# Fills on GpSimd, the bound of v from TensorE, one bank for the column products of w_in, and a written-out order made anew

## The chip, the core and the metric

The kernel runs on one core of a Trainium2 chip. The metric is the device time of one execution in microseconds (us), the median of three runs. The profile is of one further execution of the same program.

The engines are TensorE (PE in the profile; PEld its weight loads), VectorE (DVE), ScalarE (ACT), GpSimd (POOL) and SyncE (SP), which issues most DMAs. Each runs its own list of instructions strictly in order and waits for others by semaphores.

## The reference, cut to what matters

```
# q, k, v: 4 x 8 heads x 576 x 64
out_d  = softmax(q_d @ k_d.T / 8) @ v_d     # q_d, k_d, v_d: means over groups of 4 positions
local  = softmax(q @ k.T / 8, |i - j| < 4) @ v
x      = repeat(out_d, 4) + local           # 2304 tokens x 512
g      = relu(x @ w_in) ** 2                # w_in 512 x 2048
y      = g @ w_out                          # w_out 2048 x 512
logits = y @ w_gate + log1p(exp(y @ w_noise)) * noise
out    = sum over the two best of 8 experts e of weight * relu(y @ w1[e]) @ w2[e]
```

`w_in` and `w_out` come as 8-byte floats and are turned into 4-byte ones on the chip. Every product is made of 2-byte halves: each operand is scaled by a power of two and split into a high and a low fp16 part, and three products (high-high, high-low, low-high) are added. The scale needs a bound of the operand's size, so that nothing overflows: for x a bound from v (a mean of rows of v can't be larger than v), for w_in a bound of its columns, for w_out one of its norm.

## The kernel before, in words

A table `ORDER` of some 1100 short names sets the program: each name is a step with its number, `start` says which function it calls, and the steps are issued in the table's order. So each engine's list is the table's order, cut down to what each step puts on that engine.

The part of the program ahead of the first product of x with w_in is called **the start** here. It holds

- `constants()`: masks, identity matrices (`idf`, `idb`) and zero fills (`pms`, `pTs`, `vws`; VectorE, lines 159 to 162);
- units of attention, 8 for each of the 4 sequences. A unit loads `qkT` (step `qk`), sums groups of four (`G`, VectorE, L268), makes scores (`S` and `D`, TensorE, L295 and L310), takes maxima (`ml`, `md`, VectorE), exponentials (`el`, `ed`, ScalarE), sums and divisions (`nl`, `nd`; for the first sequence the multiplications of `nd` are GpSimd's), transposes (`PT`, TensorE and ScalarE), multiplies by v (`PW`, tile `px`, TensorE, then VectorE `xt` L448), and splits x (`xb`, tile `xall`);
- v's groups (`vg` loads, `vm` bounds, `vs` sums). `vm` for all sequences is two squares with a running sum on ScalarE (L215), 0.63 us each; `Xa`, `Xm`, `Xb` make the scale of x from it;
- the eight pieces of w_in: load (`il`), ScalarE (`ia`, L530), VectorE (`ib`, L538), ScalarE (`ic`, L542), VectorE (`ij`, L547), then the products of column blocks with themselves on TensorE (`in`, L1065) into four PSUM banks, `pn` twice and `pm` twice; four reductions on VectorE (`is`, L1071) and one over their results (`wS`, L1075) give the bound, `wT` and `wU` the scale `s_in`;
- the split of w_in into `wih` (`wh`, ScalarE, L1088) and `wil` (`wl`, VectorE, L1095), eight column blocks of each;
- the eight pieces of w_out in the same way; their norm is read by `os`: eight products of column blocks with themselves (L1120) and a multiplication by the identity with a sum (VectorE, L1121), then `of` (tile `pfr`).

Then come 72 steps `M` (x times w_in, tile `ph`, 24 matmuls each, L617), of which eight belong to one chunk of 256 tokens, and `Y` (g times w_out, tile `y`); the first chunk's are in quarters, `yh` and `yl`. Attention units 4 and later of the table, the gate of each of 18 tiles of 128 tokens (`ga` to `gg`) and the scatter of its rows lie between them. A gate is `ga`, `gb` (row of y), `gc` (its transpose), `gd` (logits, tile `pl`, TensorE), `gf` (some twenty small VectorE instructions: `gate_d2`, `gate_d3`, `gate_d4`), `ge` (ranks, tile `pr`, TensorE, which needs `ohs`, a late result of `gf`) and `gg`. The steps `cm` (tile `phc`, L932) and `cw` (`po`, L948) are the first expert's products, `pe` the preparation of the experts' weights; the loop over the experts 1 to 7 follows.

Of the kernel before, what the change touches and what calls it, by code (L numbers as in the profile page):

```python
# [26 lines left out]
P = 128  # L27
# [25 lines left out]
vg0 vg3 ob0 qk0 vg2 S0 vg1 vm0 qk1 qk2 vm1 vm2 G0 S1 ml0 G1 D0 md0 ml1 el0 vg4 ed0 S2 vm3 G2 vm4 el1 D1 il0 Xa0  # L53
md1 Xm0 nl0 nd0 D2 vw0 vs4 ed1 ia0 md2 PT0 nl1 ed2 nd1 ib0 Xb0 ml2 qk3 ic0 el2 G3 S4 vs0 il1 nl2 ia1 il2 ij0 PT1
nd2 ib1 PW0 il3 ic1 D4 S3 ia2 md4 ml3 il4 vw1 vs1 ed4 D3 el3 md3 ia3 il5 PT2 il6 ml4 S5 el4 ib2 ij1 ib3 D5 nl3
md5 vw2 nl4 in0 nd4 ed3 S6 xb0 in1 ia4 nd3 ic3 il7 ib4 PW1 ij3 ol2 D6 ic2 ij2 md6 in2 ic4 xb1 ia5 ij4 vs2 PT3
ib5 ia6 ic5 ib6 vs3 ml5 vw3 PW2 ol3 in3 ij5 ic6 ol0 xb2 vg5 ia7 ij6 vw4 in4 ib7 PT4 ic7 in5 oa2 is3 ij7 in6 ed5
oB2 PW3 in7 oa3 is7 el5 oc2 wS0 ml6 wT0 ol1 oj2 wU0 xb3 oa0 wh1 oB0 oB3 vw5 nl5 wh5 wl1 oc0 oj0 wh0 wl0 os0 wh3
oc3 oj3 oa1 qk4 oB1 os2 wl5 wh2 wl3 wh6 wh7 os3 el6 M5 oc1 oj1 qk5 wl7 ed6 of3 ra5 os1 wh4 nl6 M0 wl6 wl4 vm5
wl2 S7 r0 of1 PW4 nd5 oh2 oo2 ol5 oh3 oh0 vs5 oo3 M1 ra1 ol6 oh1 oo0 G4 D7 M4 ol7 PT5 xb4 nd6 yh0 yl9 M3 r4 md7  # L60
ra3 PW5 yl1 yl0 yh9 oa5 M6 oa6 oo1 yl13 oB5 ml7 ol4 xb5 r6 yl8 yl11 yl3 oa7 S8 yl12 PT6 yl4 ed7 el7 oB6 vg6 M2
oB7 yh6 yh8 ml8 oc5 nl7 yh4 M7 oj5 yh13 oc6 D8 oc7 oj6 yh11 oj7 yh3 oa4 vm6 yh1 oB4 os7 os5 yh14 vw6 md8 yl14
# [37 lines left out]
def moe_kernel(ctx, tc, qk_in, vwin, vgrp, w_in, w_out, w_gate, w_noise, noise, w1, w2, out):  # L100
# [940 lines left out]
    def win_pieces():  # L1041
# [343 lines left out]
```

## Time and profile before

| | |
|---|---|
| three runs | 974.52, 974.89, 978.32 us, median 974.89 |
| the profiled execution | 974.24 us, its span 972.5 us |
| TensorE busy | 916.3 us, 94% of the span |
| VectorE busy | 580.7 us, 60% |
| ScalarE busy | 498.9 us, 51% |
| GpSimd busy | 132.4 us, 14% |
[...]

The span runs from the first instruction to the last one in the trace; the execution's own time is 1.7 us longer. Busy shares are means over stages with different limits.

### The profile page before, as it was taken

Reading aid. Unit: us, or ns where it says so; the run is one execution under the profiler, and the core shown is the slowest. Engines: PE = TensorE matmul, PEld = TensorE weight load, DVE = VectorE, ACT = ScalarE, POOL = GpSimd, SP = SyncE. Lnnn points to the kernel's source line nnn. Section 1 sums busy time; section 2 is a strip of 40 time slices with the busy share of each in tenths; the row PEclk is TensorE's granted clock in tenths of the full one; section 3 lists DMA queues with packets and bytes.
Section 4 is the critical chain, followed back from the end, with each engine's and each line's share of the span. In section 5 each row is a group of like instructions: output and inputs, shape, how many; then the busy total and the mean of one; then the engine's idle time right before and its main releaser. Section 6 shows DMA issues by size and latency. Waiting matters only on the chain.

```text
span 972.5 us, 20336 instructions
## 1 busy us (share of the span) xinstructions
PE 916.3 (94%) x8278; PEld 619.0 (64%) x8278; DVE 580.7 (60%) x1812; ACT 498.9 (51%) x1076; POOL 132.4 (14%) x151
## 2 busy tenths in 40 slices
PE   4549999999999899999999979999999999999997
PEld 2437988675766567676757546746565565656574
DVE  7989887488678666566477765543435262626221
ACT  5688767455466455455744472753626263624010
POOL 2501100011102010010111121020111111110203
PEclk9768999999999999999999999999999999999999
DMA  9942587923241502013411748771847667590304
GB/s 290 337 147 97 169 262 287 240 90 86 88 101 58 86 30 49 21 61 96 161 56 36 226 122 222 122 206 20 221 56 204 73 187 90 158 119 10 43 1 55
DMA packets 103143, 121.17 MB, mean 125 GB/s; under 512 B 68256, under 2 KB 68448, under 8 KB 100992
## 3 DMA queue, kind: packets, MB, share of 16 engines
q1 hardware_dynamic: 94544, 100.30, 38.0%
q0 software_dynamic: 8496, 19.48, 10.0%
q8 instruction: 67, 1.10, 0.5%
q14 instruction: 36, 0.29, 0.1%
HBM read 70.33 MB, written 35.02 MB: 108 GB/s over the span
## 4 chain that ended last, share of the span: by engine, by line
PE 65%; DVE 4%; ACT 2%; DMA 1%; issue 0%; POOL 0%; POOLq 0%; ACTq 0%; DVEq 0%
PE po L948 20%; PE phc L932 19%; PE y L663 11%; PE ph L617 11%; DMA xs<-row,si 1%; ACT xall L861 1%; PE px L429 1%; PE px L421 1%; PE pol L975 1%; PE S L310 0%; PE S L295 0%; PE pfr L479 0%; PE ptp L375 0%; PE pl L740 0%; ACT r L636 0%
## 5 line engine op out<-in xcount | busy, mean ns | idle before, releaser
L617 PE MATMUL ph<-xall,wih 128*128 128x256 f16 x1152 | 196.1, 276 | 0.6 <-ACT r L636 0.4
L932 PEld LDWEIGHTS <-we 128*128 128x128 f16 x1536 | 148.5, 98 | 50.7
L948 PE MATMUL po<-we,h 128*128 128x512 f16 (+1 forms) x816 | 177.3, 379 | 0.0
L617 PE MATMUL ph<-xall,wil 128*128 128x256 f16 x576 | 158.6, 275 | 2.0 <-DVE wil L1095 2.0
L932 PE MATMUL phc<-xT,we 128*128 128x384 f16 (+1 forms) x1152 | 150.6, 293 | 0.0
L948 PEld LDWEIGHTS <-h 128*128 128x128 f16 (+1 forms) x816 | 83.4, 102 | 91.2
L663 PE MATMUL y<-wo,gh 128*128 128x512 f16 x448 | 133.3, 379 | 0.0
L617 PEld LDWEIGHTS <-wih 128*128 128x128 f16 x1152 | 111.1, 99 | 18.4 <-issue 1.9
L934 ACT ACTIVATE h<-phc 128x384 f16<-128x384 f32 (+1 forms) x112 | 47.3, 423 | 135.3 <-PE phc L932 135.3
L950 DVE TENSOR_SCALAR ob<-po,om 128x512 f32<-128x512 f32 (+1 forms) x34 | 25.5, 749 | 122.8 <-PE po L948 122.8
L832 POOL DMA_INDIRECT xs<-row,si x36 | 38.6, 1072 | 403.1 <-issue 110.3
L951 POOL DMA_INDIRECT out_dram<-ob,tk x34 | 52.3, 1538 | 298.6 <-DVE ob L950 284.2
L935 DVE SCALAR_TENSOR_TENSOR h<-phc,h 128x384 f16<-128x384 f32 (+1 forms) x112 | 52.2, 470 | 64.9 <-ACT h L934 64.9
L663 PE MATMUL y<-wo,gl 128*128 128x512 f16 x224 | 84.9, 379 | 0.3 <-DVE gl L646 0.3
L663 PEld LDWEIGHTS <-gh 128*128 128x128 f16 x448 | 42.1, 98 | 44.6 <-issue 1.0
L646 DVE TENSOR_TENSOR gl<-g,gh 128x512 f16<-128x512 f32 x64 | 44.3, 693 | 39.7 <-ACT gh L645 39.3
L617 PEld LDWEIGHTS <-wil 128*128 128x128 f16 x576 | 56.9, 99 | 9.8 <-DVE wil L1095 2.5
L636 ACT ACTIVATE r<-ph 128x512 f32<-128x512 f32 x72 | 42.2, 586 | 13.2 <-PE ph L617 13.0
L640 ACT ACTIVATE g<-r 128x512 f32<-128x512 f32 x72 | 45.4, 630 | 2.3
L861 ACT ACTIVATE junk<-w1raw 128x1024 bf16<-128x1024 f32 x24 | 25.4, 1056 | 36.4 <-DMA w1raw<-in_moe_w_dram 25.8
L878 DVE SCALAR_TENSOR_TENSOR we<-w1raw,sce,we 128x1024 f16<-128x1024 f32 x32 | 40.6, 1278 | 2.7 <-ACT we L877 2.7
L878 DVE SCALAR_TENSOR_TENSOR we<-w2raw,sce,we 128x1024 f16<-128x1024 f32 x32 | 40.6, 1275 | 0.9 <-ACT we L877 0.9
(354 smaller groups left out, 1382.3 us busy)
## 6 DMA issues: line engine op xcount, KB each, us to landing
w1raw<-in_moe_w_dram SPq DMA_DIRECT2D x8, 2048.0 KB
w2raw<-in_moe_w_dram SPq DMA_DIRECT2D x8, 2048.0 KB
xs<-zrow SPq DMA_DIRECT2D x8, 1290.0 KB
qkT<-in_qk_dram SPq DMA_DIRECT2D x16, 579.0 KB
raw<-in_moe_w_out_dram SPq DMA_DIRECT2D x8, 1024.0 KB
out_dram<-zrow SPq DMA_DIRECT2D x1, 4864.0 KB
raw<-in_moe_w_in_dram SPq DMA_DIRECT2D x4, 1024.0 KB
vw<-in_vwin_dram SPq DMA_DIRECT2D x48, 76.0 KB
```

The lines of the kernel that those rows point to most:

```text
L617: nc.tensor.matmul(ph[:, f], a[:, kk, fo], bb[:, kk], start=(n == 0), stop=(n == 11))
L636: nc.scalar.activation(r, ph, AF.Relu, scale=KAPPA)
L640: nc.scalar.activation(g, r, AF.Square)
L646: nc.vector.tensor_tensor(gl, g, gh, op=OP.subtract)
L663: nc.tensor.matmul(py[c, tt], a[:, o], bb[:, ft], start=(ft == 0 and n == 0), stop=(ft == 15 and n == 2))
L832: st = nc.gpsimd.indirect_dma_start(out=xs, out_offset=bass.IndirectOffsetOnAxis(ap=si[:, kk:kk + 1], axis=0), in_=roww, in_offset=None)
L878: nc.vector.scalar_tensor_tensor(wl[:, o], raws[i][:, o], ss[i], wh[:, o], op0=OP.mult, op1=OP.subtract)
L932: nc.tensor.matmul(ph[:, :n], a[:, fo], xT[:, bb], start=(i == 0), stop=(i == 11))
L934: nc.scalar.activation(hh[:, f], ph[:, :n], AF.Relu)
L935: nc.vector.scalar_tensor_tensor(hl[:, f], ph[:, :n], 0.0, hh[:, f], op0=OP.max, op1=OP.subtract)
L948: nc.tensor.matmul(po, a[:, f, jo], bb[:, do], start=(i == 0), stop=(i == 23))
L951: st = nc.gpsimd.indirect_dma_start(out=out, out_offset=bass.IndirectOffsetOnAxis(ap=tk[:m], axis=0), in_=ob[:m], in_offset=None, compute_ ...
```

## The change

Six things change.

1. The zero fills of `pms[1]`, `pTs` and `vws` are GpSimd's.
2. For the first sequence, `vm` is eight matmuls on TensorE: the upper halves of v's 4-byte words, read as 2-byte floats, in blocks of 128 columns times themselves, added up in one bank `pv0`, 32 matmuls in all. The largest element bounds v. The other sequences keep ScalarE's squares. `x_scale(0)` reduces `pv0` instead of `vmx`.
3. w_in's 64 products of column blocks go into one bank `pn`, on top of each other, and one reduction reads it (`is7`; the other `is` do nothing). `wS` has no reduction left.
4. w_out's norm per piece is the largest element of the products (one reduction) in place of the sum of the diagonal.
5. `gf` of the tiles 0 to 15 is three steps, `gx`, `gy`, `gz`, so that other steps can stand between.
6. `ORDER` is new from the first name to the last.

```diff
-vg0 vg3 ob0 qk0 vg2 S0 vg1 vm0 qk1 qk2 vm1 vm2 G0 S1 ml0 G1 D0 md0 ml1 el0 vg4 ed0 S2 vm3 G2 vm4 el1 D1 il0 Xa0
+qk0 vg0 G0 qk1 S0 S1 ml0 D0 G1 il0 el0 nl0 vg2 qk2 D1 ml1 md0 ed0 vm0 nd0 vg4 md1 ia0 vg1 el1 S2 ed1 ib0 S4 G2
...
         nc.gpsimd.memset(pms[0], 0.0)
+        for i in range(2):
+            nc.gpsimd.memset(pTs[i][0], 0.0)
+            nc.gpsimd.memset(vws[i][32:64], 0.0)
...
-        nc.vector.memset(pms[1], 0.0)
-        for i in range(2):
-            nc.vector.memset(pTs[i][0], 0.0)
-            nc.vector.memset(vws[i][32:64], 0.0)
+        nc.gpsimd.memset(pms[1], 0.0)
...
+    pv0 = ps1.tile([P, 512], F32, tag="m1", name="pv0")
+    seen_v = [0]
+
     def vg_max(b, hp):
+
         vg = vgs[b, hp]
-        for i in range(2):
...
+        if b:
+            for i in range(2):
...
+            return
+        v = vg.rearrange("g a b -> g (a b)").bitcast(BF16).rearrange("g (f n w) -> g f n w", n=P, w=2)[:, :, :, 1]
+        for f in range(8):
+            nc.tensor.matmul(pv0[:, :P], v[:, f], v[:, f], start=(seen_v[0] == 0), stop=(seen_v[0] == 31))
+            seen_v[0] += 1
...
-        nc.vector.tensor_reduce(m1, vmx[b], AX.X, OP.max)
+        nc.vector.tensor_reduce(m1, vmx[b] if b else pv0[:, :P], AX.X, OP.max)
...
-                nc.tensor.matmul(pn[i][:, P * (f % 4):P * (f % 4) + P], v[:, f], v[:, f], start=i in fresh,
-                                 stop=done_[i] == 16)
-                fresh.discard(i)
+                done_[0] += 1
+                nc.tensor.matmul(pn[:, P * (f % 4):P * (f % 4) + P], v[:, f], v[:, f], start=done_[0] == 1,
+                                 stop=done_[0] == 64)
 
         def peak(c):
-            for i in (2 * c, 2 * c + 1):
-                nc.vector.tensor_reduce(top[:, i:i + 1], pn[i], AX.X, OP.max)
+            if c:
+                nc.vector.tensor_reduce(top, pn, AX.X, OP.max)
...
-                nc.vector.scalar_tensor_tensor(pq[:, P:2 * P], pq[:, :P], 1.0, idf, op0=OP.mult, op1=OP.mult,
-                                               accum_out=acc[q_][:, c:c + 1])
+                nc.vector.tensor_reduce(acc[q_][:, c:c + 1], pq[:, :P], AX.X, OP.max)
```

Three places of the new order. First SyncE's list, the program's first loads (`wih` here is v's groups of the first sequence, four loads; `raw` a piece of w_in; `vw` v for the windows). Before:

```order
L206 DMA wih_168<-in_vgrp_dram 72x1024 x2
L251 DMA qkT0_0_186<-in_qk_dram 128x1158
L206 DMA wih_168<-in_vgrp_dram 72x1024 x2
L251 DMA qkT0_1_213<-in_qk_dram 128x1158
L251 DMA qkT0_2_215<-in_qk_dram 128x1158
L206 DMA vg1_0_262<-in_vgrp_dram 72x1024
L526 DMA raw_296<-in_moe_w_in_dram 128x2048
L258 DMA vw0_96<-in_vwin_dram 38x512 x2
L251 DMA qkT0_3_350<-in_qk_dram 128x1158
L526 DMA raw_380<-in_moe_w_in_dram 128x2048
```

And now:

```order
L264 DMA qkT0_0_178<-in_qk_dram 128x1158
L209 DMA wih_166<-in_vgrp_dram 72x1024
L264 DMA qkT0_1_183<-in_qk_dram 128x1158
L539 DMA raw_229<-in_moe_w_in_dram 128x2048
L209 DMA wih_166<-in_vgrp_dram 72x1024
L264 DMA qkT0_2_234<-in_qk_dram 128x1158
L209 DMA vg1_0_261<-in_vgrp_dram 72x1024
L209 DMA wih_166<-in_vgrp_dram 72x1024
L271 DMA vw0_96<-in_vwin_dram 38x512 x2
L264 DMA qkT0_3_340<-in_qk_dram 128x1158
L209 DMA wih_166<-in_vgrp_dram 72x1024
L539 DMA raw_428<-in_moe_w_in_dram 128x2048
```

The first `qkT` stands ahead of all of v's groups, the first piece of w_in is fourth and no longer tenth, and the last of v's groups comes after the fourth `qkT`.

Second VectorE's list around the scale of w_in (`s_in`): `vi` is a finished piece of w_in, `raw` a piece of w_out, `pm0_90` and `S` attention. Before:

```order
L547 SCALAR_TENSOR_TENSOR vi_162<-xall_144 128x1024
L538 SCALAR_TENSOR_TENSOR raw_592<-raw_592 128x1024
L448 TENSOR_TENSOR xt_739<-px_726,od_740 128x256
L1071 TENSOR_REDUCE top_167<-pm0_165 128x1
L1071 TENSOR_REDUCE top_167<-pm1_166 128x1
L1075 TENSOR_REDUCE cm__756<-top_167 128x1
L323 TENSOR_REDUCE mx_760<-S_533 128x5
...
L238 TENSOR_REDUCE xm2_763<-pmx_758 1x1
L547 SCALAR_TENSOR_TENSOR raw_592<-raw_592 128x1024
L173 TENSOR_SCALAR es_769<-pmx_758 128x1
L174 TENSOR_SCALAR s_in_145<-es_769 128x1
```

And now:

```order
L551 SCALAR_TENSOR_TENSOR xall_145<-xall_145 128x1024
L560 SCALAR_TENSOR_TENSOR vi_163<-xall_145 128x1024 x2
L484 SCALAR_TENSOR_TENSOR xall_145<-xt_678,sx0_469,xall_145 128x256
...
L1080 TENSOR_REDUCE top_165<-pn_164 128x1
L551 SCALAR_TENSOR_TENSOR raw_618<-raw_618 128x1024
L251 TENSOR_REDUCE xm2_780<-pmx_754 1x1
L551 SCALAR_TENSOR_TENSOR raw_620<-raw_620 128x1024
L175 TENSOR_SCALAR es_787<-pmx_754 128x1
L176 TENSOR_SCALAR s_in_146<-es_787 128x1
```

Two bank reductions, the reduction over them and one unit's maxima are gone from between the last `vi` and `s_in`; a piece of w_out (`raw_620`) has come in.

Third TensorE's list around the last two gates (`pl` logits, `pty` the last row's transpose, `phc` 12 matmuls of the first expert, `pr` ranks, where `ohs` is what VectorE delivers). Before:

```order
L740 MATMUL pl_8382<-wgs_149,yT_8370 128x16
...
L932 MATMUL phc_8401<-wih_168,we0_7835 128x384
...
L728 MATMUL pty_8481<-idh_101,row_8357 128x128
...
L932 MATMUL phc_8495<-wih_168,we0_7835 128x384
...
L740 MATMUL pl_8510<-wgs_149,yT_8480 128x16
...
L800 MATMUL pr_8529<-ohs_8459,trib_103 128x8
...
L932 MATMUL phc_8552<-wih_168,we0_7835 128x384
...
L932 MATMUL phc_8608<-wih_168,we0_7835 128x384
...
L800 MATMUL pr_8624<-ohs_8602,trib_103 128x8
...
L932 MATMUL phc_8650<-wih_168,we0_7835 128x384
```

And now:

```order
L753 MATMUL pl_8389<-wgs_150,yT_8377 128x16
...
L945 MATMUL phc_8408<-wih_166,we0_7748 128x384
...
L741 MATMUL pty_8455<-idh_101,row_8364 128x128
...
L945 MATMUL phc_8472<-wih_166,we0_7748 128x384
...
L945 MATMUL phc_8502<-wih_166,we0_7748 128x384
...
L753 MATMUL pl_8517<-wgs_150,yT_8454 128x16
...
L945 MATMUL phc_8552<-wih_166,we0_7748 128x384
...
L813 MATMUL pr_8567<-ohs_8492,trib_103 128x8
...
L945 MATMUL phc_8581<-wih_166,we0_7748 128x384
...
L945 MATMUL phc_8626<-wih_166,we0_7748 128x384
...
L945 MATMUL phc_8641<-wih_166,we0_7748 128x384
...
L813 MATMUL pr_8656<-ohs_8620,trib_103 128x8
```

Between `pty` and the last `pl` stand two `phc` where there was one, and between the last `pl` and the last `pr` four where there were two.

## Rows read from the trace of the kernel before

**Rows 1.** the page: busy time of each engine.

```profile
PE 916.3 (94%) x8278; PEld 619.0 (64%) x8278; DVE 580.7 (60%) x1812; ACT 498.9 (51%) x1076; POOL 132.4 (14%) x151
```

**Rows 2.** who waited for whom, TensorE, 79 to 545 us: total us, times, longest.

```profile
PE S L310 <- DVE pm L321: 2.9, 2, 2.7
```

**Rows 3.** the same view, 545 to 600 us.

```profile
PE pr L800 <- DVE ohs L786: 2.9, 1, 2.9
PE pl L740 <- ACT yT L729: 2.5, 1, 2.5
```

**Rows 4.** VectorE in order of time: start, duration, operation [idle before it].

```profile
9.16 1.34 DVE L268 TENSOR_REDUCE qkT<-qkT 128x288 f32<-128x1152 f32 x1
...
27.64 1.34 DVE L538 SCALAR_TENSOR_TENSOR raw<-raw 128x1024 int32<-128x1024 int32 x1 [0.73 <-ACT raw L530]
...
46.14 2.30 DVE L538 SCALAR_TENSOR_TENSOR wil<-wil 128x1024 int32<-128x1024 int32 x1
...
63.79 0.15 DVE L174 TENSOR_SCALAR s_in<-es 128x1 int32<-128x1 int32 x1
...
74.10 2.48 DVE L1095 SCALAR_TENSOR_TENSOR wil<-vi,s_in,wih 128x1024 f16<-128x1024 f32 x2
```

**Rows 5.** busy time by stretch: engines, then granted clock, DMA share, GB/s.

```profile
5.60:9.00 3.40, 0.81 (x34) 0.61 (x33) 2.69 (x5) 0.51 (x2) 0.00 (x0) 1.00 1.02 295
37.90:49.10 11.20, 4.95 (x62) 3.77 (x62) 11.13 (x13) 6.71 (x10) 10.97 (x8) 0.65 0.90 306
75.44:79.20 3.76, 3.76 (x18) 2.70 (x19) 3.47 (x5) 2.37 (x7) 0.00 (x0) 0.50 0.05 18
```

**Rows 6.** ScalarE in order of time.

```profile
26.39 1.22 ACT L530 ACTIVATE raw<-raw,lob 128x1024 int32<-128x1024 uint32 x1 [3.06 <-DMA raw<-in_moe_w_in_dram]
```

**Rows 7.** VectorE by groups, 27.6 to 63.9 us: busy us, mean ns, idle before.

```profile
L448 DVE TENSOR_TENSOR xt<-px,od 128x256 f32<-128x256 f32 x4 | 1.7, 419 | 0.3 <-ACT od L447 0.3
L333 DVE TENSOR_REDUCE nb<-S 128x2 f32<-128x288 f32 (+1 forms) x4 | 1.6, 410 | 0.6 <-PE S L310 0.6
...
L324 DVE TENSOR_TENSOR pm<-S,mx 128x190 f32<-128x190 f32 (+1 forms) x4 | 1.4, 346 | 0.4
L323 DVE TENSOR_REDUCE mx<-S 128x5 f32<-128x190 f32 (+1 forms) x4 | 1.3, 337 | 0.2 <-ACT pd L344 0.2
L1071 DVE TENSOR_REDUCE top<-pn 128x1 f32<-128x512 f32 x2 | 1.3, 683 | 0.0
```

**Rows 8.** GpSimd in order of time.

```profile
0.95 0.36 POOL L136 MEMSET pm<- 128x320 f32 x1
```

**Rows 9.** TensorE in order of time.

```profile
75.44 0.40 PE L617 MATMUL ph<-xall,wil 128*128 128x256 f16 x1 [2.00 <-DVE wil L1095]
...
79.82 1.10 PE L1120 MATMUL pq<-raw 128*128 128x128 bf16 x8
```

**Rows 10.** chain that ended last: start, length, single steps of attention units.

```profile
278.87 0.51 PE S L295 x39
279.37 0.64 PE S L310 x8
...
317.35 0.43 PE px L421 x8
...
318.24 0.38 PE px L432 x8
...
338.22 0.36 PE ptd L383 x4
```

**Rows 11.** TensorE in order of time, around the last two gates.

```profile
550.10 6.01 PE L932 MATMUL phc<-wih,we 128*128 128x384 f16 x36
...
568.27 0.17 PE L800 MATMUL pr<-ohs,trib 128*128 128x8 bf16 x1 [2.88 <-DVE ohs L786]
```

**Rows 12.** ScalarE in order of time, the same place.

```profile
559.90 1.00 ACT L729 COPY yT<-pty 128x1024 f16<-128x1024 f16 x1
...
576.98 1.06 ACT L861 ACTIVATE xall<-w2raw 128x1024 bf16<-128x1024 f32 x1
```

More of the change, by code (lines that the diff above doesn't have):

```diff
@@ L58 @@
[L58 to L62, printed above, removed]
@@ new lines @@
+in0 ia1 Xa0 md4 nl2 nd2 D3 Xm0 ed4 Xb0 md3 ib1 PT2 nl3 vw1 ml4 xb0 ed3 PW1 ia2 il3 il4 ic1 S5 is3 el4 S6 il5 D6
+nd3 PT3 il6 ib2 ij1 D5 nl4 vw2 ia3 ic2 ml5 ib3 el5 nd4 md5 ic3 vs3 il7 md6 ij2 ia4 ol2 ol3 xb1 ia5 ed6 ib4 ij3
+in1 vw3 in2 ic4 ol0 ia6 ib5 ij4 vs2 in3 ib6 ic5 PW2 ic6 ol1 ij5 nl5 ia7 PT4 ml6 in4 ib7 ic7 ij6 ij7 xb2 in5 in6
+in7 ed5 oa2 nd5 oa3 is7 oB2 wS0 el6 S7 wT0 qk4 oB3 oc2 wU0 oc3 wh7 oj2 oj3 PW3 vw4 wh2 wl7 wh3 os3 os2 D7 wl2
+xb3 wl3 oa1 of3 oB1 qk5 ob0 vg5 wh0 wh6 qk6 nl6 wl0 wh4 wh5 PW4 wl5 oa0 PT5 S9 oc1 M0 oB0 wl4 wl6 wh1 wl1 oj1
@@ new lines @@
+vw12 nd13 el14 pf7 gb0 md15 M17 md14 nl14 ra16 PT13 M23 ed14 ga1 gc0 vw13 vs8 Y8 qk8 vg9 ml15 Y9 PW12 Y10 gd0
+gb1 ed15 vm9 Y11 vw14 el15 qk9 S16 gx0 gy0 gz0 nd14 xb12 PW13 G9 Y12 gc1 Y13 ra23 ge0 xb13 qk10 gg0 ra17 Y14 gd1
+M22 G8 PT14 vw15 M20 gx1 gy1 gz1 vs9 PW14 vg10 vw16 ge1 gg1 D16 Y15 S17 ra22 nl15 ra20 nd15 M21 D17 vm10 ga2
+md16 vs10 PT15 ga3 vg11 ml16 el16 M18 gb2 ip1 ra18 ed16 vm11 G10 ml17 Y16 gb3 nl16 Y17 xb14 nd16 md17 PW15 Y18
+ra21 el17 qk11 S18 xb15 Y19 D18 ed17 gc2 gd2 gc3 nl17 PT16 gx2 gy2 gz2 G11 nd17 M27 ra27 S19 Y20 md18 vs11 gd3
@@ new lines @@
+PW25 PT26 nd27 ml28 ra41 D29 M44 md28 el28 md29 xb25 M47 gb9 vw27 PT27 vw26 ed29 gb8 ml29 ed28 nl28 PW26 vw28
+gc8 Y40 ra44 el29 xb26 Y41 Y42 PW27 S30 xb27 Y43 nd28 D30 ra47 nl29 gd8 Y44 PT28 md30 gx8 gy8 gz8 vw29 nd29 Y45
+gc9 gd9 M48 gx9 gy9 gz9 ge8 S31 gg8 M49 ra49 Y46 ed30 ge9 PW28 Y47 D31 ml30 ra48 ga10 PT29 gg9 el30 md31 M51
+gb10 M50 nl30 xb28 gc10 ml31 nd30 ra51 ra50 ga11 PW29 el31 M53 gb11 M55 xb29 gd10 Y48 ra53 PT30 M52 ed31 nl31
+Y49 gc11 nd31 ra55 Y50 ra52 vw30 gd11 vw31 Y51 gx10 gy10 gz10 PT31 Y52 gx11 gy11 gz11 PW30 xb30 M54 PW31 ge10
@@ L96 @@
+cm2 gx16 cm7 gc17 gy16 cm0 gz16 le1 cm1 gd17 gx17 cm6 ge16 gy17 cm5 gg16 gz17 cm4 cm3 ge17 gg17 pe17 pe18 pe19
+pe20 cw1 pe21 pe22 pe23 pe24 cw0 lr1 pe25 pe26 pe27 cw2 pe28 pe29 pe30 cm8 cm11 pe31 cm12 cm9 cm10 pe32 cm13
+pe33 cm14 lr2 le2 cm15 cw4 cw3
 """
@@ L198, in load_vg @@
             vd[b] = ap.tile([72, NP, 4, 64], F32, tag="vd", name=f"vd{b}")
+        if hp == 0 and b:
             vmx[b] = ap.tile([P, H], F32, tag="vmx", name=f"vmx{b}")
@@ L1042, in win_pieces @@
         vi = wx.tile([P, 4, FF], F32, tag="wo", name="vi")
-        pn = [ps1.tile([P, 512], F32, tag="m1", name=f"pn{i}") for i in range(2)]
-        pn += [ps2.tile([P, 512], F32, tag="m2", name=f"pm{i}") for i in range(2)]
-        top = sp.tile([P, 4], F32, name="top", bufs=1)
-        fresh = set(range(4))
-        done_ = [0] * 4
+        pn = ps1.tile([P, 512], F32, tag="m1", name="pn")
+        top = sp.tile([P, 1], F32, name="top", bufs=1)
+        done_ = [0]
         wih = wp.tile([P, 4, FF], F16, tag="wih", name="wih")
@@ L1062, in gram @@
             for f in range(8):
[L1063 to L1067 removed]
+                done_[0] += 1
+                nc.tensor.matmul(pn[:, P * (f % 4):P * (f % 4) + P], v[:, f], v[:, f], start=done_[0] == 1,
+                                 stop=done_[0] == 64)
         def peak(c):
[L1070 to L1071 removed]
+            if c:
+                nc.vector.tensor_reduce(top, pn, AX.X, OP.max)
         def scale():
[L1074 to L1076 removed]
+            W["mx"] = across(top)
         def scale1():
```

76 lines of the change are left out of this document (30 added, 46 removed).

## The prediction

> **What bounds the kernel now.** I read the busy times first [rows 1]: TensorE works 916.3 of 972.5 us, so 56 us are all that any order of the work can win. The next question is where they lie, and the view of waits answers it. From 79 to 545 us TensorE waits for next to nothing; the one group worth a row is 2.9 us in two waits [rows 2]. From 545 to 600 us, around the last gates, two single waits make 5.4 us: 2.9 for the ranks, 2.5 for the last row's transpose [rows 3]. Nearly all the rest lies in the start. So behind the start the end moves with TensorE's list: what is done sooner, or out of that list, comes off the end.
>
> The start is VectorE's. The first product of x with w_in gets its second half of the operands at 75.44 us, after 2.00 us of waiting for `wil`, VectorE's split of w_in [rows 9]. In VectorE's rows the reader can follow what that split waits for: the first sum of a `qkT` at 9.16, the second piece of w_in at 27.64, the scale `s_in` at 63.79 (done at 63.94), and the split in question as the first of the pair at 74.10, done near 75.3 [rows 4]. Between 27.64 and 63.94 VectorE has hardly a gap: the groups of that stretch show about 2 us of idle time in all beside their busy time, the largest at a maximum that waits for `S` [rows 7].
>
> **The fills, and the first loads.** Five fills kept VectorE busy for 2.69 us between 5.6 and 9.0 us [rows 5]. GpSimd has nothing then; a fill of 128x320 takes it 0.36 us [rows 8], so by size the four larger ones take some 2.5 us and are over near 4 us, long before anything reads those tiles. With the first `qkT` also first in SyncE's list, I expect VectorE's first sum at 5.5 to 7 us, not 9.16. But that gain is met further on. ScalarE sat 3.06 us until the second piece of w_in landed at 26.39 [rows 6], and VectorE's 27.64 stands on that. Ahead of this load both lists hold the same bytes (four `qkT`, five groups of v, a piece of w_in, a `vw`), so it lands when it did. I cost the early start at nothing by itself: what it gives is room, 3.4 us, for work that came later. Bounds: the load lands 2 us sooner because less is queued beside it, or VectorE comes 1 us late.
>
> **From the second piece to the scale of w_in.** The lists of both kernels have the same sixteen large steps of weights here. Gone are three of four bank reductions at 0.68 us and the small one over them, 2.0 us together with overlaps. Done before 27.6 instead are one pair of `ml` steps (0.34 and 0.35), two `md` (0.41 and about 0.15 of its scaling) and two `xt` (0.42): 2.6 us [rows 7]. Added are one sum and one division of another unit, 0.8 us. Net 3.8 us less. Against it stands GpSimd: while it worked for 10.97 of 11.2 us, VectorE's steps were stretched, one of w_in to 2.30 us where its like at 27.64 took 1.34 [rows 4, 5]. Measured against unstretched steps of the same form I put the loss at 3 to 3.5 us in that stretch, 0.3 us for each us of GpSimd. One more `nd` (1.2 us on GpSimd) now falls ahead of the scale: 0.4 us back. **3.4 us sooner** at `s_in`.
>
> **From the scale to the first product.** Before, eight large steps at about 1.2 us each stand on VectorE from `s_in` to the needed `wil`, three of them splits; now seven, four of them splits, and more small ones (a norm's four). That is a draw but for the wait in it; I take 0.4 us. The start is over **3.8 us** sooner (1.5 to 6).
>
> The eight squares of v on ScalarE are no term: it is idle there, as its 3.06 us show. The 32 matmuls that replace them cost at most four times the 1.10 us of an eight [rows 9], and lie in time in which TensorE has under two thirds of its work; uncovered they would be 4.4 us. The new norm of w_out (one reduction for a multiplication with a sum) is the same length to 0.1 us.
>
> [...]
>
> **Work moved into the start.** Counting TensorE's list ahead of the first product, there are now two more `S`, one more `D`, one more transposition and one more `px`, and eight products of w_out fewer. Prices at full clock [rows 10]: `S` 0.51, `D` 0.64, the transposition two pieces like the one of 0.36, `px` three pieces from 317.35 to 318.62, 1.27. That is 1.02 + 0.64 + 0.72 + 1.27 = 3.65, less 1.0 for the eight products [rows 9]. TensorE does it while it would wait for VectorE, and has **2.7 us** less afterwards. [...]
>
> **The last gates.** Before, ScalarE's evacuation of the last row's transpose (`yT`, 559.90) stood behind an exponential of the gate before, which waited for VectorE; TensorE waited 2.5 us for it [rows 3, 12]. Now it stands ahead of that, and two `phc` steps, not one, follow the transpose; a `phc` is 2.0 us (three in 6.01 [rows 11]). The transpose ends near 554.7, `yT` near 556, and TensorE comes to the last `pl` at 558.8: no wait. Between the last `pl` and the last `pr` there were two `phc`, 4.0 us, and 2.88 of waiting to 568.27 [rows 11]. Now four, 8.1 us, so TensorE comes there at 567.3. VectorE's chain from the last logits to `ohs` took 6.4 us and gets a little longer by one more evacuation and the other gate's ranks; it is done near 567.5. What was done at 572.2 is done at 567.7: **4.5 us**. What is late next is the norm of the second expert's weights: eight squares on ScalarE of 1.06 us and a read each [rows 12], some 9.4 us that now begin near 568.9 and end at 578.3, as before. But TensorE has two first-expert products of 5.2 us to do ahead of it where it had one, so the wait stays under half a us. Bounds 2 and 5.4.
>
> **The middle.** `gf` in three steps and the new table move every wait of the steady stage. TensorE's list holds about the same, and between a gate's logits and its ranks the middle tile has 11 us of TensorE's work, as before. I keep the 2.9 us [rows 2] as they are; it may lose them, or gain 4.
>
> **Sum**, against the profiled execution's 974.2 us, which lies 0.7 under the median of the runs shown: 974.2 - 3.8 - 2.7 - 4.5 = 963.2, say 963.
>
> **The rivals.**
> - The start gains nothing: GpSimd's extra work or a later load eats the 3.8 us. For it: VectorE's stretched steps, and the load at 26.39 that sets the pace. Against: the reductions are gone whatever happens. 974.2 - 2.7 - 4.5 = 967.0.
> - The last gates gain nothing: the added evacuations on VectorE push `ohs` back as far as TensorE's list was filled. For it: those evacuations stand between the gate's own steps in VectorE's list. Against: each is about half a us, and the filling is 4 us. 974.2 - 3.8 - 2.7 = 967.7. With both of these, 971.5.
> - Slower: the split gates. A gate's three parts now let other steps of VectorE in between, and TensorE stands still at `pr` if `ohs` is late. Sixteen tiles have it; the change turns into a loss when the mean wait passes 11.0 / 16 = 0.7 us, and into one that can be measured at 1.0 us. At 1.5 us it gives 963.2 + 24 = 987. For it: the last tile's 2.88 us, with 4 us of TensorE's work in between [rows 11]. Against: only two of the sixteen have less than 6 us now, and none with over 5.6 us waited before.
>
> **How the numbers follow.** The forecast has 0.64, the start's rival 0.13, the last gates' 0.11, both together 0.05, the split gates 0.07. The forecast's own range is 957 to 968, from the bounds of its terms. For all cases: at best 6.0 + 3.6 + 5.4 + 2.9 comes off, 956.3; at the other end I go to 971.5, which holds both failures. About 0.5% (4.9 us) is what a measurement here can tell from no change; below 970.0 counts as faster. That is the forecast nearly whole and most of the two single rivals, 0.82; same 0.12; slower 0.06.
>
> **What would show it.** The first `qkT` sum before 7 us; `s_in` near 60.5; the first whole product near 71.6; TensorE's waits from 545 to 600 us under 1.5 us in all; no wait of `pr` for `ohs` above 1 us in the middle. It is wrong if `s_in` stays at 63, if the first products stay at half clock for more than 5 us, or if the middle shows new waits of `S`, `D` or `pr` of over 5 us.

## The result, and the profile after

The changed kernel takes 988.13 us (985.64 to 990.50, three runs) where the kernel before takes 974.89: a ratio of 1.0102 with a 95% interval of 1.0074 to 1.0130. It is slower by some 10 to 13 us; 963 was forecast. The profiled execution is that of 985.64 us, span 983.9, so 11.4 us over the profiled one of before.

The first view is the busy times, which answer to [rows 1].

```profile
PE 928.9 (94%) x8310; PEld 628.8 (64%) x8310; DVE 578.6 (59%) x1794; ACT 493.6 (50%) x1060; POOL 131.9 (13%) x156
```

TensorE has 32 matmuls more, the bound of v (4.2 us), and is busy 12.6 us longer. Where that and the rest lie is told by stretches: up to the first product of x with w_in, its first 3.8 us, to 545, to 600, to the end. The first cut is 75.44 before, where the product got its second half, and 76.40 after, where its first matmuls start. The columns are those of [rows 5] (engines, granted clock, DMA share, GB/s). First before:

```profile
0.00:75.44 75.44, 35.94 (x514) 26.15 (x515) 64.43 (x131) 53.58 (x99) 20.80 (x27) 0.78 0.75 251
...
79.20:545.00 465.80, 461.68 (x5140) 334.43 (x5138) 331.51 (x1261) 267.60 (x666) 44.49 (x76) 1.00 0.38 111
545.00:600.00 55.00, 49.16 (x337) 30.56 (x336) 36.69 (x133) 28.05 (x50) 8.98 (x10) 1.00 0.69 183
600.00:973.00 373.00, 365.77 (x2274) 225.17 (x2272) 144.56 (x286) 147.35 (x256) 58.18 (x38) 1.00 0.53 108
```

And after:

```profile
0.00:76.40 76.40, 46.93 (x659) 35.96 (x660) 63.70 (x127) 50.10 (x94) 23.36 (x34) 0.78 0.76 264
76.40:80.30 3.90, 3.90 (x24) 2.80 (x20) 3.90 (x4) 2.93 (x3) 0.00 (x0) 0.50 0.04 16
80.30:545.00 464.70, 450.05 (x4948) 326.67 (x4947) 320.21 (x1232) 258.08 (x648) 38.52 (x70) 0.99 0.37 105
545.00:600.00 55.00, 53.85 (x343) 30.87 (x341) 34.96 (x129) 28.08 (x49) 9.96 (x14) 1.00 0.62 160
600.00:984.00 384.00, 374.16 (x2349) 232.55 (x2346) 155.80 (x306) 154.43 (x269) 60.09 (x39) 1.00 0.54 112
```

TensorE's rows at the cut:

```profile
76.40 0.61 PE L630 MATMUL ph<-xall,wih 128*128 128x256 f16 x2
76.80 0.42 PE L630 MATMUL ph<-xall,wil 128*128 128x256 f16 x1
```

So the second half of the product comes at 76.80, 1.36 us later than before.

TensorE's idle time and its work give the whole account. The stretch ahead of the cut is 0.96 us longer. TensorE's busy time from the cut on is 928.9 - 46.9 = 882.0 us, where it was 916.3 - 35.9 = 880.4: 1.6 more, of which 0.4 are the product's first matmuls, which stood ahead of the cut before. Idle in the middle: 464.70 - 450.05 = 14.65 against 465.80 - 461.68 = 4.12, 10.5 more. From 545 to 600: 1.15 against 5.84, 4.7 less. After 600, up to each span's end at 983.9 and 972.5: 9.7 against 6.7, 3.0 more. The sum is 0.96 + 1.6 + 10.5 - 4.7 + 3.0 = 11.4.

The view of who waited for whom names these waits (80 to 545, 545 to 600 and from 600 on, the counterpart of [rows 2] and [rows 3]):

```profile
PE px L442 <- DMA vw<-in_vwin_dram: 8.6, 3, 4.5
PE ph L630 <- ACT r L649: 1.5, 3, 1.1
...
PE pr L813 <- DVE ohs L799: 1.1, 1, 1.1
...
PE phc L945 <- DVE xall L948: 3.0, 1, 3.0
```

The 2.9 and 2.5 us at the last gates are gone. In their place stand three waits for loads of `vw`, v for the windows, in the middle, and one of `phc` for VectorE at 600 us. The longest of them in TensorE's list, in order of time:

```profile
129.55 1.12 PE L442 MATMUL px<-pT,vw 102*64 102x64 f32 x16 [4.53 <-DMA vw<-in_vwin_dram]
```

SyncE's list in order of time, from 120 us:

```profile
119.96 0.90 SPq L271 DMA_DIRECT2D vw<-in_vwin_dram  x3
```

And two stretches, while an earlier such load ran nearly alone and just after the wait:

```profile
110.00:114.00 4.00, 4.00 (x60) 3.95 (x58) 3.07 (x4) 3.82 (x9) 0.00 (x0) 1.00 0.14 47
130.00:135.00 5.00, 5.00 (x59) 4.82 (x56) 3.30 (x9) 2.33 (x6) 0.00 (x0) 0.50 0.46 142
```

The load that `px` needs at 125 us was issued at 120 and landed at 129.5. Its buffer had been free since about 99 us, when the unit before it on that buffer was done. SyncE's list shows why it was not issued then; after, and then before, at the same place:

```
L271 DMA vw0_96<-in_vwin_dram 38x768
L271 DMA vw0_96<-in_vwin_dram 38x512 x3
L271 DMA vw1_97<-in_vwin_dram 38x768
L271 DMA vw1_97<-in_vwin_dram 38x512
...
L258 DMA vw0_96<-in_vwin_dram 38x768
L258 DMA vw0_96<-in_vwin_dram 38x512
...
L258 DMA vw1_97<-in_vwin_dram 38x768
L258 DMA vw1_97<-in_vwin_dram 38x512
L258 DMA vw0_96<-in_vwin_dram 38x512 x2
```

The last two loads of `vw0` belong to a unit behind, and their buffer is read until 119.9 us (`px` of the unit at 118.6). Now they stand ahead of the load of `vw1`, so SyncE waits there with the one that is needed first behind them. The wait also costs clock: TensorE then works for 5 us, from 130 to 135, at the granted clock 0.50 (1.00 in the kernel before), by which 2.5 us of work are lost, an estimate from that row.

VectorE in the start, in order of time (compare [rows 4]):

```profile
0.98 3.00 DVE L147 TENSOR_SCALAR pm<-pm 128x1 f32<-128x1 f32 x5
...
7.63 1.34 DVE L281 TENSOR_REDUCE qkT<-qkT 128x288 f32<-128x1152 f32 x1
...
29.76 1.23 DVE L551 SCALAR_TENSOR_TENSOR raw<-raw 128x1024 int32<-128x1024 int32 x1
...
63.36 0.16 DVE L176 TENSOR_SCALAR s_in<-es 128x1 int32<-128x1 int32 x1
```

The first sum is 1.5 us sooner and not 2.2 or more, the second piece of w_in 2.1 us later, `s_in` 0.4 us sooner. VectorE's work between those two, from the start of the second piece to the end of `s_in`, before and after (VectorE's busy time is the third of the five):

```profile
27.64:63.94 36.30, 19.10 (x288) 14.64 (x280) 33.58 (x54) 28.11 (x52) 14.18 (x11) 0.69 0.72 248
29.76:63.52 33.76, 18.53 (x275) 14.37 (x275) 29.87 (x46) 25.83 (x46) 10.96 (x10) 0.70 0.79 281
```

Its busy time fell by 3.7 us, its idle time rose by 1.2.

### The profile page after: what moved, and what is told of

It reads as the page before. It is cut to its first block, busy times and chain, and to the rows that moved or that the text cites. A ratio compares the mean times of both kernels' runs of the same rounds, so it can differ in the third digit from the quotient of the medians.

```text
span 983.9 us, 20370 instructions
## 1 busy us (share of the span) xinstructions
PE 928.9 (94%) x8310; PEld 628.8 (64%) x8310; DVE 578.6 (59%) x1794; ACT 493.6 (50%) x1060; POOL 131.9 (13%) x156
## 4 chain that ended last, share of the span: by engine, by line
PE 44%; DVE 3%; DMA 1%; ACT 1%; issue 1%; SPq 0%; POOL 0%; POOLq 0%; ACTq 0%
PE po L961 19%; PE phc L945 18%; PE y L676 3%; PE ph L630 3%; DMA xs<-row,si 1%; PE pol L988 1%; DVE we L891 1%; ACT xall L874 0%; DMA mt<-xs 0%; DVE wil L948 0%; PE pfr L492 0%; SPq L913 0%; ACT wih L947 0%; DVE oh L797 0%; ACT row L731 0%
## 5 line engine op out<-in xcount | busy, mean ns | idle before, releaser
L630 PE MATMUL ph<-xall,wih 128*128 128x256 f16 x1152 | 193.8, 274 | 1.5 <-ACT r L649 1.5
```

Of the source, the lines that this page charges most:

```text
L630: nc.tensor.matmul(ph[:, f], a[:, kk, fo], bb[:, kk], start=(n == 0), stop=(n == 11))
```

## The experiments

The ratios are to the kernel before on the same chip. It took 974.6, 977.9, 978.5, 974.0 and 974.4 us on the five chips used, so sizes are compared on one chip, and between chips only roughly. Times of single steps are those of one profiled execution: the changed kernel, profiled a second time (e16_after), had `s_in` at 64.66 and not 63.36, so a step of one us between two profiles tells little by itself.

**The code under the old order, and the loads in the middle.** First chip, with the next three.

```diff
-(ORDER of the change)
+(ORDER of before; gf0 to gf15 as gx gy gz in place)
```

> Parts 1 to 5 of the change under the order of before (the three steps of a split gate stand where the one step stood). Theory A, that the new order is what costs: 970 to 976 us, like before or a little below, since three reductions of 0.68 us are gone; TensorE waits for no vw load after 80 us. Theory B, that the code parts cost (the fills on GpSimd hold up VectorE's first additions, 3.00 us where they took 0.98; the 32 matmuls for the bound of v hold up TensorE): 980 us or more.

975.01 us, 1.0002 (0.9991 to 1.0014): theory A. The code parts together cost and gain nothing. `s_in` comes at 64.03, though three reductions of 0.68 us less stand ahead of it; VectorE's waits from 28 to 64 us show where the room went:

```profile
DVE vi L560 <- ACT xall L555: 1.2, 1, 1.2
DVE raw L560 <- ACT raw L555: 1.0, 1, 1.0
```

VectorE now waits 1.2 us for ScalarE's step of a piece of w_in, a wait that it didn't have before.

```diff
-vg6 vw6 os6 ... vw8 ... vw7
+vg6 vw6 vw7 os6 ... vw8
-PW20 ... vw22        -vw26 (six names ahead of its px)
+PW20 vw22            +PW24 vw26
```

> The changed kernel with three names of the order moved: the loads vw7, vw22 and vw26 are issued as soon as their buffer is free. Theory A, that they waited behind other loads in SyncE's list: the three waits of px for vw (4.5, 2.8 and 1.2 us) go, and with them the half clock at 130 to 135 us (2.5 us) and in part that at 345 to 350: 975 to 980 us. Rival, that the transfers themselves are slow and land late from anywhere: less than 3 us gained, 985 or more.

978.45 us, 1.0037 (1.0022 to 1.0052): theory A. That is 9.7 us under the changed kernel by the medians, 6 to 11 by the ratios (1.0102, and 1.0155 in e16_after). `px` waits for `vw` 1.6 us after 80. But the first product came at 78.75 in this execution, and the start shows a wait of the same kind at an earlier unit:

```profile
34.14 1.12 PE L442 MATMUL px<-pT,vw 102*64 102x64 f32 x16 [3.06 <-DMA vw<-in_vwin_dram]
```

**The fills and the bound of v.**

```diff
-        nc.gpsimd.memset(pms[1], 0.0)
+        nc.vector.memset(pms[1], 0.0)
+        (pTs and vws the same)
```

> The changed kernel with the fills of pms[1], pTs and vws back on VectorE. Theory A, that the fills only set VectorE's first 8 us: the five additions take 1 us again and not 3, the fills 2.7 us, the first sum of a qkT comes at 8 to 9 us, the scale of w_in within 1 us of 63.4, the time within 2 us of the changed kernel. [...]

989.10 us, 1.0153 (1.0121 to 1.0185): as changed. VectorE's first rows:

```profile
0.97 0.99 DVE L144 TENSOR_SCALAR pm<-pm 128x1 f32<-128x1 f32 x5
...
9.17 1.34 DVE L281 TENSOR_REDUCE qkT<-qkT 128x288 f32<-128x1152 f32 x1
```

Without GpSimd's fills the five additions take 0.99 us and not 3.00. The first sum then comes 1.5 us later, and the end doesn't move by more than the chips differ (988.13 and 988.37 with the fills on GpSimd). `s_in` was at 66.04 here, 2.7 us later than in the changed kernel's first profile, which misses theory A's 1 us; e2_vw with the fills on GpSimd had 65.72, so the fills needn't be the cause.

```diff
-            vm for b = 0: 32 matmuls into pv0
+            vm for b = 0: ScalarE's squares into vmx, as before
```

> The changed kernel with the bound of the first sequence's v by ScalarE's squares, as before. Theory A, that the 32 matmuls delay TensorE's scores, for which VectorE waits between 20 and 40 us (6.4 us idle there, 2.5 in before): VectorE's idle time there falls under 4.5 us, the second piece of w_in starts before 28.5 us (29.8 now), s_in comes near 61.5 and the end 1.5 to 3 us sooner. Rival, that ScalarE's eight squares (5 us) then hold up its exponentials as much: s_in at 63 or later, the time the same or longer.

986.27 us, 1.0116 (1.0088 to 1.0143): the rival. VectorE's second piece came at 31.50, `s_in` at 64.61.

**The start's load, and the last gates.** Second chip.

```diff
 (e2_vw)
-vw0 ... vw1 (four names ahead of its px)
+vw0 vw1
```

> e2_vw with one more load moved: vw1 is issued right behind vw0, ahead of two pieces of w_in. Theory A, that the start is late for the same reason as the middle (in e2_vw px waited 3.06 us at 34.14 for vw1, issued at 15.55 to 17.25 behind two pieces of w_in, and ScalarE's third piece stood behind that px): that wait is under 0.5 us, VectorE's third piece of w_in (36.67 in e2_vw) starts before 34.5, the first product of x with w_in before 77 (78.75), the time 975 to 976.5 where e2_vw had 978.5. Rival, that all loads share one rate and the pieces land as much later: third piece and time as in e2_vw, 978 or more.

980.72 us, 1.0024 (1.0009 to 1.0038). Theory A fell: the fourth `qkT` sum slipped to 28.40 (23.21 in e2_vw), for which VectorE waited 7.03 us, the second piece to 35.28, the first product to 81.27. By its ratio the time is that of e2_vw.

```diff
 (e5_vw1)
-gx17 cm6 ge16 gy17 cm5 gg16 gz17 cm4 cm3 ge17 gg17 pe17 pe18 pe19 pe20 cw1
+gx17 cm6 pe17 ge16 gy17 cm5 pe18 gg16 gz17 cm4 pe19 cm3 ge17 gg17 pe20 cw1
```

> e5_vw1 with the pieces pe17 to pe20 (norm of the second expert's weights) back between the last gates' steps, as before. Theory A, that the late pieces made VectorE late at 600 us: the wait of phc for xall (2.9 us) falls under 0.5, the waits of pr stay near 1.1: 2 to 3 us less than e5_vw1. Rival, that the pieces there hold up the last gates: pr waits 2 us more, the same time as e5_vw1.

981.59 us, 1.0038 (1.0025 to 1.0051): neither. `pr` waits 1.1 us as in e5_vw1, and `phc` waits 4.5 us where it waited 2.3, more and not less.

```diff
-(ORDER of the change)
+(e1_code's up to ga17; then the change's from lr0 on)
```

> e1_code (order of before) with the changed kernel's order from lr0 on, thus the last gates alone. Theory A: TensorE's waits from 545 to 600 us fall from 5.9 to about 1.2 us, and the wait of phc for xall of 3 us comes in: 973 us, 1.8 below e1_code's 975.0. The prediction's own step said 4.5 us less: 970.5. Rival: the gates gain nothing here, 975.

977.93 us, 0.9994 (0.9981 to 1.0006): nothing gained, as the rival has it. `pr` waits 1.1 us where it waited 2.9, but `phc` waits 3.8 us, and after it TensorE ran from 595 to 605 us at 0.52 and 0.80 of its clock.

```diff
 (e7_oldstart_tail)
+(pe17 to pe20 as in e6_vw_tail)
```

> e7_oldstart_tail with pe17 to pe20 between the last gates' steps. Theory A: both gains, no wait of phc for xall: 970 to 971 us, below both kernels. Rival: the pieces on ScalarE and VectorE hold up the ranks by as much, 973 or more.

979.74 us, 1.0020 (1.0008 to 1.0033): theory A fell again, `phc` waits 4.3 us. VectorE's rows of this kernel gave the cause:

```profile
580.20 0.75 DVE L963 TENSOR_SCALAR wil<-po,om 128x512 f32<-128x512 f32 x1 [4.43 <-PE po L961]
585.14 0.23 DVE L929 SCALAR_TENSOR_TENSOR om<-mt 128x2 f32<-128x2 f32 x2 [4.19 <-DMA mt<-xs]
...
586.19 0.15 DVE L176 TENSOR_SCALAR sce<-es 128x1 int32<-128x1 int32 x1
...
587.56 2.48 DVE L891 SCALAR_TENSOR_TENSOR we<-w1raw,sce,we 128x1024 f16<-128x1024 f32 x2 [0.39 <-ACT we L890]
```

`om` is part of `lr1`, which now stands ahead of `pe25`. VectorE stands 4.2 us at it for a DMA, and the scale `sce` of the second expert, whose operands were there, waits behind it; so do both engines' splits. The changed kernel has the same row, with `sce` 1.05 us behind it:

```profile
595.25 0.24 DVE L929 SCALAR_TENSOR_TENSOR om<-mt 128x2 f32<-128x2 f32 x2 [2.83 <-DMA mt<-xs]
```

**lr1 moved.** Third chip.

```diff
 (e7_oldstart_tail)
-cw0 lr1 pe25 pe26 pe27 cw2
+cw0 pe25 pe26 pe27 lr1 cw2
```

> e7_oldstart_tail with one name moved: lr1 (rows for the first expert, with VectorE's steps om that wait for a DMA) stands behind pe25 to pe27, as before, and no longer ahead of them. Theory A, that VectorE stood 4.2 us at om for that DMA with the scale sce of the second expert behind it: the wait of phc for xall (3.8 us) falls under 0.5, the waits of pr stay, the time is 3 to 4.5 us under that of before. Rival, that the norm is late through TensorE's two products ahead of pfr: the wait stays over 2 us, the time within 1.5 us of before.

971.93 us, 0.9938 (0.9921 to 0.9955): theory A, and more: 6.6 us under before, where 3 to 4.5 were expected. No wait of `phc` is left.

```diff
 (e2_vw)
-cw0 lr1 pe25 pe26 pe27
+cw0 pe25 pe26 pe27 lr1
```

> e2_vw with lr1 moved in the same way. Theory A: the wait of phc for xall (2.9 us) falls under 0.5, 2 to 3 us less than e2_vw against before, so 1 to 2 us over before. Rival: the same time as e2_vw, 3.5 us over before.

973.25 us, 0.9946 (0.9928 to 0.9965): theory A, and more. By its own median it is 5.2 us under e2_vw; the rest of the step in the ratio lies in the two chips.

```diff
-(e10_vw_lr's order up to Y8)
+(before's order up to Y8; then e10_vw_lr's names that are left)
```

> The order of before up to the first chunk's end (the name Y8, near 145 us), then the changed order with vw22, vw26 and lr1 moved. Theory A, that of the new order only the start (3 us late) and the blocked loads and steps cost: the first product as in before, TensorE's waits from 150 to 545 us under 5 us, no wait of phc: 3 to 5 us under before and 4 to 6 under e10_vw_lr. Rival, that the middle of the new order costs by itself: within 1.5 us of before or above.

977.23 us, 0.9987 (0.9978 to 0.9996). This tells nothing of the middle: where the two orders are joined TensorE got a new wait of 4.1 us for ScalarE's `r`.

```diff
 (e10_vw_lr)
-il1 el3 il2 ... vw1
+vw1 il1 el3 il2
```

> e10_vw_lr with vw1 issued ahead of the second piece of w_in (behind qkT_3 and v's groups, where e5_vw1 had it ahead of them and the fourth qkT sum slipped to 28.4 us). Theory A, that px's wait for vw1 (3.06 us in e2_vw) sets the third piece: the fourth qkT sum stays at 21 to 24, that wait is under 0.5 us, the third piece (36.67 in e2_vw) starts before 35, the first product 1.5 to 3 us before that of e10_vw_lr. Rival, that the loads share one rate: the second piece comes as much later, and the first product within 1 us of e10_vw_lr.

973.23 us, 0.9941 (0.9922 to 0.9959): the rival. The wait for `vw1` is down to 0.6 us, but ScalarE waits for the second piece of w_in instead, and `s_in` comes at 65.05 in both, the first product at 78.07 and 78.10.

```profile
31.34 1.19 ACT L543 ACTIVATE raw<-raw,lob 128x1024 int32<-128x1024 uint32 x1 [4.41 <-DMA raw<-in_moe_w_in_dram]
```

**The shares, on one chip.** Fourth chip; e13_lr is the changed kernel with `lr1` moved, e16_after the changed kernel.

```diff
-cw0 lr1 pe25 pe26 pe27
+cw0 pe25 pe26 pe27 lr1
```

> The changed kernel with lr1 behind pe25 to pe27 and nothing else. Theory A: phc's wait for xall (3.0 us) and what half clock follows it go: 3 to 6 us under e16_after. Rival, that lr1 counts for little by itself and the loads did it: less than 2 us under e16_after.

984.04 us, 1.0091 (1.0066 to 1.0115): theory A, 4.3 us under e16_after.

```diff
 (e10_vw_lr)
-PW1 ia2
+ia2 PW1
```

> e10_vw_lr with ScalarE's first step of the third piece of w_in (ia2) ahead of the evacuation od of the second unit, which waits for px and its window load. Theory A, that this wait sets the pace of the start: the third piece on VectorE (35.94 in e10_vw_lr) starts before 34.5, s_in (65.05) 1 us or more sooner, the first product (78.10) near 76.5. Rival, that the load itself or VectorE's later list sets it: third piece and s_in within 0.5 us of e10_vw_lr.

972.98 us, 0.9987 (0.9972 to 1.0003): the rival. Third piece at 35.66, `s_in` 65.44.

```diff
 (e10_vw_lr)
-PW4 wl5 oa0 PT5 S9 oc1 M0
+PW4 wl5 oa0 oc1 M0 PT5 S9
```

> e10_vw_lr with the transposition PT5 and the scores S9 behind M0 and not ahead of it. Theory A, that TensorE's added unit (2.3 us of waiting for xt and 1.6 us of work at half clock) holds up the first product: it starts 2 to 3.5 us sooner than the 78.10 of e10_vw_lr, and the time falls by 1 to 3 us. Rival, that VectorE's split wil sets it anyway: less than 1 us.

973.30 us, 0.9984 (0.9968 to 0.9999): the rival, the time is that of e14_ia2. The first product starts at 75.42, 2.7 us sooner than in e10_vw_lr, but it then stands still for its second half, as in the kernel before:

```profile
78.08 0.39 PE L630 MATMUL ph<-xall,wil 128*128 128x256 f16 x1 [2.05 <-DVE wil L1102]
```

That half was at 78.50 in e10_vw_lr. (`s_in` was at 67.14 in this execution and at 65.05 in e10_vw_lr; from there to the second half it is 10.94 us, where e10_vw_lr has 13.45.) The added unit's work is done behind the product instead.

> The changed kernel again, beside the other three on one chip: 1.0 to 1.3% over before, 8 us or more over e10_vw_lr's ratio to before.

988.37 us, 1.0155 (1.0129 to 1.0180), more over before than the 1.0 to 1.3% expected. With e14_ia2 beside it the three loads and `lr1` (and `ia2`, which moved nothing) are worth 15.4 us on this chip.

**The window loads themselves.** Fifth chip. All loads of `vw`, in the same places, each as two:

```diff
-            nc.sync.dma_start(vt[h0:h0 + KW, :n] ..., vwin[b, hp, :, t0:t0 + n] ...)
+            for r0, r1 in ((0, 32), (32, KW)):
+                nc.sync.dma_start(vt[h0 + r0:h0 + r1, :n] ..., vwin[b, hp, r0:r1, t0:t0 + n] ...)
```

> The changed kernel with each load of v's windows (38 rows) issued as two, 32 rows and 6 rows; order and all else as changed. Theory A, that such a load runs on two DMA engines of 16 (share 0.14 of them busy, 47 GB/s while it ran alone) and that this makes it late and holds back that part of every later load on these two: the waits of px for vw (8.6 us) fall under 4, the second piece of w_in on VectorE comes at or before 29.8, s_in before 63, and the time is 6 us or more under the changed kernel's (1.0102 to 1.0155 of before), so at most 1.007. Rival, that the place in SyncE's list alone makes them late, and twice as many DMAs cost more issue time: waits as before, 1.010 or more.

975.29 us, 1.0006 (0.9990 to 1.0021): theory A, 13 us under the changed kernel by the medians, 9 to 15 by the ratios, with its order untouched. `px` waits for `vw` 0.2 us after 80; `phc` still waits 4.2 us, which is `lr1`'s. The second piece of w_in comes at 29.14, `s_in` at 62.16, the first product at 75.19 (its second half at 75.60).

```diff
 (e10_vw_lr)
+(the split of e17_rows)
```

> e10_vw_lr with the window loads split in the same way. Theory A: the start comes sooner, the first product at 76 or before (78.10 in e10_vw_lr), 2 to 4 us under e10_vw_lr, which had 0.9946 and, with ia2 moved, 0.9987 of before. Rival: the same as e10_vw_lr, or more by the added issues.

967.80 us (966.97 to 970.13), 0.9936 (0.9914 to 0.9958): theory A, below both kernels. `s_in` is at 62.16 again, the first product at 75.21 (its second half at 75.61). TensorE's waits from 80 to 545 and from 545 to 625 us:

```profile
PE ph L631 <- ACT r L650: 3.5, 3, 3.0
PE px L443 <- issue: 0.8, 1, 0.8
...
PE pr L814 <- DVE ohs L800: 1.1, 1, 1.1
```

Neither e9_oldstart_tail_lr nor the kernel before was tried with split loads; e9_oldstart_tail_lr has the same ratio, 0.9938, without them and with the old start and middle.

## Why the prediction was wrong

**The middle is the step that failed.** The prediction kept its 2.9 us "as they are", with bounds of -2.9 and +4 (the +4 isn't in the upper end of its range, 971.5), and argued from TensorE's list alone. Measured were 10.5 us more of idle time, 8.6 of them in three waits for `vw`, and 2.5 us of clock behind the first. The loads of those units stand in SyncE's list, which the prediction read for the start only. There the waits' cause can be seen beforehand: a load that waits for a buffer ahead of one that doesn't. e2_vw shows it (6 to 11 us less for three names). e17_rows shows that the load's slowness is the other half of the cause: with faster loads in the same places the waits are gone too (0.2 us where 8.6 were). The prediction's signs of being wrong named new waits of `S`, `D` and `pr` there, not of `px`.

**The last gates** were right in size and wrong in what follows. TensorE's idle time from 545 to 600 us fell by 4.7, forecast 4.5. "What is late next" was named as the norm's squares on ScalarE, with under half a us of waiting. What was late was the scale behind it: VectorE stood at `om` for a DMA. That took 3.0 us back, and in some of the kernels' profiles clock as well (0.52 from 595 to 600 us in e7_oldstart_tail); e13_lr prices `lr1` at 4.3 us and e7 and e9, on different chips, at 0.6% of the time. The prediction listed TensorE's and ScalarE's steps there, not VectorE's.

**The start** failed as well. The second half of the first product was forecast 3.8 us sooner and came 1.36 later in the profiled execution (76.80); with the same start the product began not at 76.4 but at 77.7 to 79.5 in e2_vw, e10_vw_lr, e13_lr and e16_after. `s_in`, forecast near 60.5, stayed at 63.36, which the prediction had named as a sign of being wrong. By its parts:

- The fills: "long before anything reads those tiles" is true, but while they ran VectorE's first five additions took 3.00 us, and 0.99 without them (e3_fills). Why they took longer beside the fills isn't shown. The 2 us came out of the 3.4 us of room that the prediction gave the early start, as far as e3_fills can tell: the end didn't move.
- The second piece of w_in was said to land when it did, "or VectorE comes 1 us late". ScalarE no longer waited for it (25.99), but VectorE had its step at 29.76, 2.1 us later. From 20 to 40 us VectorE is busy 13.4 us where it was 16.7: steps that came into this stretch wait for TensorE and ScalarE, and TensorE once 1.8 us for a `vw`.
- From there to `s_in`, 33.6 us where it was 36.15: 2.55 of the 3.4 forecast. The work was forecast rightly, VectorE is busy 3.7 us less; 1.2 us of it came back as waits, the longest 1.6 us of `xt` for ScalarE's `od`. e1_code shows the same under the old order: of what VectorE is freed there, part is waiting for ScalarE.
- From `s_in` to the product's second half 13.4 us against 11.65, so 1.8 more and not 0.4 less: TensorE waits 2.3 us for `xt` of the added unit and then does its transposition and scores at half clock (0.50 from 74 to 76.4 us), ahead of the product. In e15_m0, without this, it is 10.9 us, but the time stays: the unit's work is then done later.

What set part of the rest is shown by the two kernels with split window loads: `s_in` comes at 62.16 in both (63.4 to 67.1 in the others with this start; 68.2 in e5_vw1 and e6_vw_tail, whose `vw1` is early), the second half of the first product at 75.60 and 75.61. That is still no sooner than the 75.44 of before; what keeps the start from the forecast 71.6 stays open. The rival that "GpSimd's extra work or a later load eats" the start's gain had half of this, at 967.0.

**Work moved into the start** was to give 2.7 us. Counted from the product's second half in both kernels, TensorE has 1.2 us more to do, but 2.5 us of it come from the half clock at 130 us; about 1.3 less remains. The other half clock, from 76.40 to 80.30, is as it was in before (0.50 in both) [rows 5]. What became of the remaining 1.4 isn't settled.

**The slower rival** had the sign but not the mechanism: the split gates' waits of `pr` in the middle are 0.9 us in all. That its 987 lies near the 988.13 measured is chance.

With the loads split and `lr1` moved the order does give something: e18_vw_lr_rows is 6.6 us under before by the medians, where 11 were forecast. But e9_oldstart_tail_lr is 6.6 us under before too, with the new order of the last gates alone. So no run shows a gain from the new start and middle; what is shown is the last gates' part, once `lr1` is out of the way.

## What to carry to other kernels

An in-order list is read for what stands behind a waiting instruction, on each engine that has one, the queue that issues the DMAs among them: both losses here were an instruction that waited for something far off (a buffer, a DMA), with one behind it that was ready and needed. A moved step brings along the waits of all its instructions, on all engines. And a load that is often just late is looked at by the DMA share while it runs alone: changing its shape was worth about as much as finding it a better place. Two starts are compared at the same instruction: a product that begins sooner and then waits for its second half is not sooner.

## What the runs showed of the hardware

A load of 38 rows kept few DMA engines busy: 0.14 of sixteen, 47 GB/s, while it ran nearly alone from 110 to 114 us. That is about two, an estimate from the share (0.14 x 16 = 2.2); why it is so few isn't shown. Splitting the rows into 32 and 6 made the loads faster: in e17_rows the same loads, issued at 105.9 us (107.7 in the changed kernel), were done before 110, at a share of 0.53 and 127 GB/s from 106 on, and the DMA engines then had nothing to do:

```profile
106.00:110.00 4.00, 4.00 (x52) 3.73 (x50) 4.00 (x5) 3.98 (x11) 0.00 (x0) 1.00 0.53 127
110.00:114.00 4.00, 4.00 (x81) 3.81 (x77) 2.41 (x5) 3.19 (x8) 0.00 (x0) 1.00 0.00 0
```

In e5_vw1 and e12_vw1b_lr loads of 152 KB with 38 rows, put ahead of one of 579 KB and one of 1 MB, made the step that needs the large one some 5 us later: the fourth `qkT` sum at 28.40 us where e2_vw has 23.21, and ScalarE's step on the second piece of w_in at 31.34 where e10_vw_lr has 26.52. SyncE also issued the large load later there, the fourth `qkT` in e5_vw1 at 12.85 us and not 7.73 (e2_vw). That alone doesn't explain it: e17_rows issued it nearly as late, and VectorE had its sum at 21.09 without a wait, not at 28.40. SyncE's rows, e5_vw1 and e17_rows:

```profile
12.85 0.35 SPq L264 DMA_DIRECT2D qkT<-in_qk_dram  x1
12.21 0.35 SPq L264 DMA_DIRECT2D qkT<-in_qk_dram  x1
```

What holds the large load back behind the small one was not measured by itself.

A wait of 3 to 5 us of TensorE cost more than its length when the granted clock fell behind it: to 0.50 from 130 to 135 us after the 4.5 at 125 us, 2.5 us more, an estimate from 5 us at half clock. The length of the wait alone doesn't tell whether it falls. Behind the 2.98 us at 600 it did not fall in the changed kernel (1.00 from 605 to 610 us), where the 48 matmuls of `phc` behind it took 4.76 us; behind 2.95 us in e2_vw it did (0.66 on average from 595 to 600), and the same 48 took 6.42. TensorE's rows, the changed kernel and e2_vw:

```profile
604.75 4.76 PE L945 MATMUL phc<-xall,we 128*128 128x224 f16 x48 [2.98 <-DVE xall L948]
595.27 6.42 PE L945 MATMUL phc<-xall,we 128*128 128x224 f16 x48 [2.95 <-DVE xall L948]
```

It fell behind the 3.8 in e7_oldstart_tail too, to 0.52 from 595 to 600 us.
